# More attention chunks and the whole last x turned by DMA, with half of one FFN's second weights split again from raw

## The chip, the cores and the metric

The kernel runs on one core of one Trainium2 chip. The metric is the device time of one execution in microseconds (us), as the median of several runs.

## The reference

```python
x = A_x                                  # [1, 2048, 640], fp32
xn = layernorm(x)
qkv = (xn @ wqkv)                        # 32 heads of 20
# each position attends to itself and to 7 earlier ones, 2 apart
logits = sum(q * k[pos - 2*w]) * 20**-0.5   for w in 0..7   (masked where pos - 2*w < 0)
s = (softmax(logits) @ v) @ wo
g = silu( silu(xn @ w1) @ w2 )           # w1 640x1536, w2 1536x640
out = x + s * g
```

## The kernel before

The 2048 tokens are worked off in four groups of 512 (T = 4 tiles of 128 tokens). A group is one half of the tokens of one parity, since attention steps by two. The model width 640 is DC = 5 chunks of 128 columns, the FFN width 1536 is 12 chunks, and the heads are taken in NQ = 4 quarters of 160 columns.

Every matmul is done to fp32 accuracy: each operand is split into a high part (fp32r) and the rest (low), and three matmuls are added (high x high, low x high, high x low). So a weight unit is kept as two halves, and an activation as TH and TL (x) or OH and OL (attention output), transposed, with the contraction on the partitions.

A group passes through two phases on TensorE. The qkv phase (L960 to L962) takes quarter by quarter and chunk by chunk; one weight unit there is 4 tiles x 3 matmuls. The ffn phase has twelve up-projections (L1140 to L1142, sums in the two `rot` banks, evacuated by L1153, L1154 and L1155), twelve down-projections (L1005 and L1007, six `acc` banks, evacuated through silu into the gate by L1224), and in the middle the wo projection of the group before, whose sums L1040 multiplies with the gate; L1053 loads x again, L1054 adds it and L1056 writes the output. While a group is in its ffn phase, the x of the next is loaded (L600, and L1085 for the last use), normalized on VectorE (L607 to L619) and turned.

Attention runs beside all that on VectorE (L754 scores, L757 reduction, L770 to L783 softmax, L796 to L809 values) with help of GpSimd. Its k and v need halos, rows shifted by partitions, which SyncE (SP) copies quarter by quarter by DMA (L728), with L736 to L740 carrying rows between groups. The outputs of a group are turned in five O chunks, during the next group's qkv phase.

A chunk is turned in one of two ways. On TensorE, `split_t` transposes four tiles into a `rot` bank (L629), ScalarE writes the high part (L633, and L635 for x a whole copy), and VectorE the low part (L639). By DMA, `send` regroups the 16-bit halves of the chunk on ScalarE (L657), SP issues two DMA transposes (L662), and `join` puts the halves together on ScalarE (L670), writes the high part (L676) and the low part on VectorE (L677). The tables X_DMA and O_DMA say which chunks go by DMA for which group.

Weights come into a ring of seven slots. At its first use a unit is loaded raw in fp32 by SP (L538, into tiles XR, G or PR), split by ScalarE (L574) and VectorE (L578), and its halves are stored to DRAM (L583). Later uses load the halves through GpSimd's queue (L565).

The order of instructions on each engine comes from a list scheduler written in Python (class Weave): every operation has a cost, a due time and the tiles that it reads and writes, and the planner appends operations to the engines by these. TensorE's order is fixed by the program. `free_for(old, new)` makes the use of new names wait for that of old names where they share memory.

Of the kernel before, what the change touches and what calls it, by code (L numbers as in the profile page):

```python
# [15 lines left out]
P = 128  # L16
# [42 lines left out]
O_BACK = (), (80.0, 82.0), (80.0, 82.0), (40.0, 55.0, 60.0)  # L59
X_BY = {1: 2, 3: 0, 4: 1}  # L60
SLOW, ISSUE, SUB_LATE = 8, 2.0, 3
PACE0, PACE = -20.0, 12.0
# [3 lines left out]
STORE_Q = 1, 3  # L66
SHARED = (1, 0), (1, 2), (2, 0), (2, 2), (3, 0)
# [256 lines left out]
def local_attention_silu_ffn(ctx: ExitStack, tc: tile.TileContext, x, wqkv, wo, w1, w2, out):  # L324
# [152 lines left out]
    def store_at(u):  # L477

        return 1 + (u[0] == "wo" or u[0] == "q" and u[2] in STORE_Q)
# [29 lines left out]

    def raw_load(k):  # L510
# [12 lines left out]
        pairs = []  # L523
        if u[0] == "q":
            _, q, c = u
            whole = wqkv[c * P:(c + 1) * P, :]
            pairs.append((r.rearrange("p (k m) -> p k m", k=3), whole.rearrange("p (k m) -> p k m", k=3)[:, :, q * CQ:(q + 1) * CQ]))
        elif u[0] == "w1":
            pairs.append((r.rearrange("p (c f) -> p c f", c=DC),
                          w1.rearrange("(c p) f -> p c f", p=P)[:, :, u[1] * P:(u[1] + 1) * P]))  # L530
        else:
            m = wo if u[0] == "wo" else w2
            pairs.append((r, m[u[1] * P:(u[1] + 1) * P, :]))
        by = nc.scalar if k in BY_ACT else nc.sync

        def go():
            for to, frm in pairs:
                by.dma_start(to, frm)  # L538
        if k in BY_ACT:
            add("ACT", 0.65 * len(pairs), go, [], kr, -1, nbytes=n * P * 4)  # L540
            return
        dma(go, [], kr, n * P * 4, 1 + k if k < 2 * DC else clock[0] + 5, (0.62 if k < 2 * DC else 0.45) * len(pairs))

    def raws_due(i, k):

        while rawn[0] < len(fresh) and fresh[rawn[0]] <= i + RAW_AHEAD and raw_in.get(raw_tile(rawn[0]), -1) <= k:
            raw_load(rawn[0])
            rawn[0] += 1

    def w_load():  # L550
# [11 lines left out]
        due = clock[0]  # L562
        if what[i] == "load":
# [16 lines left out]
        if what[i] == "store":  # L580
            kept = dram.tile([P, 2, n], F32, name="half_" + "_".join(map(str, u)))
            halves[u] = kept
            dma(lambda: nc.sync.dma_start(kept, both.bitcast(F32)), [kh, kl], [("half", u)], 2 * n * P * 4, due + 25)  # L583
# [101 lines left out]

    def turn_o(c, i, by, to, at, back):
# [494 lines left out]
    def ffn_phase(g, i, ix, io):  # L1181
# [13 lines left out]
        bufs = [("buf", c, h) for c in range(DC) for h in range(2)]  # L1195
# [29 lines left out]
        if g < NG - 1:  # L1225
            turn_os(g, i, begun)

# [39 lines left out]
```

## Time and profile before

| what | value |
|---|---|
| median of the runs | 598.78 us (598.73 to 599.15) |
| profiled execution, its time | 598.41 us |
| its span | 596.3 us |
| PE, matmuls | 590.6 us busy (99%) |
| DVE | 513.3 us busy (86%) |
| ACT | 248.7 us busy (42%) |
| POOL | 168.2 us busy (28%) |
| PE L629 (chunks turned on TensorE), 20 pieces of the chain | 1.5% of the chain |
| half loads L565, w1 and w2 (640 KB each) | 72, median 7.0 us from issue to landing |

In the profile PE is TensorE, DVE is VectorE, ACT is ScalarE, POOL is GpSimd, SP is SyncE. Rows of a timeline give start, duration, engine, line, operation, output<-inputs with shapes, and in brackets how long the engine was idle before and what ended that. The span counts the profiled engines' work; the execution's own time is 2.1 us longer. TensorE ran at the full granted clock throughout.

### The profile page before, as it was taken

What the parts mean: (1) busy time and instruction counts of PE and PEld (TensorE: products, weight loads), DVE (VectorE), ACT (ScalarE), POOL (GpSimd) and SP (SyncE); (2) the same over time, 40 slices, a digit from 0 to 9 for tenths busy, and PEclk for the clock granted to TensorE, in tenths of its full rate; (3) what the DMA queues carried; (4) which work ended last, traced back from release to release, by engine and by line L of the source; (5) the groups of instructions that cost most, each with busy time, mean ns of one, the idle gap of its engine ahead of it and who ended that gap; (6) DMA issues with size and microseconds to landing.
All of it is one profiled execution on the core that took longest, in us unless ns stands there. A gap on an engine that the chain in (4) does not pass through costs nothing.

```text
span 596.3 us, 9080 instructions
## 1 busy us (share of the span) xinstructions
PE 590.6 (99%) x3443; PEld 555.9 (93%) x3443; DVE 513.3 (86%) x505; ACT 248.7 (42%) x444; POOL 168.2 (28%) x229
## 2 busy tenths in 40 slices
PE   8999999999999999999999999999999999999997
PEld 7999999999999999999999999999999999999997
DVE  6499999999799978999988996999838799998744
ACT  5437375452545223747523604443412333335230
POOL 5800102233110153442221126543121233434100
PEclk9999999999999999999999999999999999999999
DMA  9999999879999999999699999998689999797952
GB/s 295 311 295 334 296 411 402 322 252 300 271 316 326 313 257 324 239 202 239 191 319 306 303 346 304 263 208 286 211 220 283 294 320 295 227 203 215 241 185 89
DMA packets 80263, 164.21 MB, mean 275 GB/s; under 512 B 19949, under 2 KB 44237, under 8 KB 80221
## 3 DMA queue, kind: packets, MB, share of 16 engines
q1 hardware_dynamic: 60381, 83.93, 52.1%
q0 software_dynamic: 19296, 79.31, 46.5%
q8 instruction: 27, 0.44, 0.3%
q10 hardware_dynamic: 544, 0.41, 0.2%
q14 instruction: 15, 0.12, 0.1%
HBM read 107.91 MB, written 34.16 MB: 238 GB/s over the span
## 4 chain that ended last, share of the span: by engine, by line
PE 98%; DMA 0%; DVE 0%; issue 0%
PE acc L1005 23%; PE acc L1007 15%; PE acc L960 10%; PE acc L961 10%; PE acc L962 10%; PE rot L1140 9%; PE rot L1142 9%; PE rot L1141 9%; PE acc L910 2%; PE rot L629 1%; DMA xin<-in_A_x_dram 0%; PE rot L894 0%; PE rot L1123 0%; DVE st L879 0%; PE rot L853 0%; DVE gate L1091 0%
## 5 line engine op out<-in xcount | busy, mean ns | idle before, releaser
L960 PE MATMUL acc<-w,th 128*128 128x480 f32 x300 | 110.6, 369 | 0.0
L961 PE MATMUL acc<-w,tl 128*128 128x480 f32 x300 | 109.8, 366 | 0.0
L962 PE MATMUL acc<-w,th 128*128 128x480 f32 x300 | 109.8, 366 | 0.0
L1005 PE MATMUL acc<-w,sh 128*128 128x384 f32 x384 | 108.6, 328 | 0.0
L1007 PE MATMUL acc<-w,sh 128*128 128x256 f32 x384 | 104.7, 273 | 0.0
L754 DVE TENSOR_TENSOR pr<-q,kv 128x2560 f32<-128x2560 f32 x32 | 90.2, 2819 | 15.9 <-DMA kv<-carry 12.7
L796 DVE TENSOR_TENSOR pr<-q,kv 128x2560 f32<-128x2560 f32 x32 | 91.5, 2860 | 1.4 <-DVE l L757 0.5
L1140 PE MATMUL rot<-th,w 128*128 128x512 f32 x240 | 91.8, 383 | 0.0
L1141 PE MATMUL rot<-tl,w 128*128 128x512 f32 x240 | 91.0, 379 | 0.0
L1142 PE MATMUL rot<-th,w 128*128 128x512 f32 x240 | 91.0, 379 | 0.0
L757 DVE TENSOR_REDUCE l<-pr 128x128 f32<-128x2560 f32 x32 | 89.7, 2804 | 0.2
L1153 ACT ACTIVATE sh<-rot 128x512 fp32r<-128x512 f32 x48 | 28.8, 599 | 134.2 <-PE rot L1142 134.1
L565 POOL DMA_DIRECT2D w<-half_w x72 | 39.0, 542 | 156.6 <-PE acc L1007 57.6
L1007 PEld LDWEIGHTS acc<-w,sh 128*128 128x128 f32 x384 | 73.7, 192 | 0.6
L1005 PEld LDWEIGHTS acc<-w,sh 128*128 128x128 f32 x384 | 72.6, 189 | 0.6
L565 POOL DMA_DIRECT2D w<-half_q x52 | 28.0, 538 | 119.8 <-PE acc L962 74.3
L962 PEld LDWEIGHTS acc<-w,th 128*128 128x128 f32 x300 | 56.7, 189 | 4.0
L960 PEld LDWEIGHTS acc<-w,th 128*128 128x128 f32 x300 | 56.7, 189 | 3.9
L961 PEld LDWEIGHTS acc<-w,tl 128*128 128x128 f32 x300 | 56.7, 189 | 3.9
L1005 PE MATMUL acc<-w,sl 128*128 128x384 f32 x192 | 55.9, 328 | 0.0
L1155 DVE TENSOR_TENSOR sl<-sf,sh 128x512 fp32r<-128x512 f32 x48 | 39.3, 819 | 16.8 <-ACT sf L1154 16.8
L1007 PE MATMUL acc<-w,sl 128*128 128x256 f32 x192 | 52.3, 273 | 0.0
(110 smaller groups left out, 1070.0 us busy)
## 6 DMA issues: line engine op xcount, KB each, us to landing
w<-half_w POOLq DMA_DIRECT2D x72, 640.0 KB, 7.0
w<-half_q POOLq DMA_DIRECT2D x52, 480.0 KB, 5.8
half_w<-w SPq DMA_DIRECT2D x24, 640.0 KB
half_q<-w SPq DMA_DIRECT2D x20, 480.0 KB
kv<-kv SPq DMA_DIRECT2D x15, 560.0 KB
w<-half_wo POOLq DMA_DIRECT2D x10, 640.0 KB, 5.6
kv<-kv SPq DMA_DIRECT2D x15, 420.0 KB
gate<-in_B_w_dram SPq DMA_DIRECT2D x16, 320.0 KB
```

Source lines behind the costliest of these rows:

```text
L565: add("POOL", 1.0, lambda: nc.gpsimd.dma_start(both, src), [("half", u)], [kh, kl], due + 10, nbytes=2 * n * P * 4)
L754: dve(2560, lambda: nc.vector.tensor_tensor(out=PR, in0=win(qq[:, t:t + 2, :], W, 0), in1=win(kv[:, 0, t:t + 2, :], W, CQ), op=OP.mult), h ...
L757: dve(2560, lambda: nc.vector.tensor_reduce(out=l[:, t:t + 2].rearrange("p t w h -> p (t w h)"), in_=PR.rearrange("p t w (h d) -> p (t w h ...
L796: dve(2560, lambda: nc.vector.tensor_tensor(out=PR.rearrange("p t w (h d) -> p t (w h) d", d=DH), in0=e[:, t:t + 2].rearrange("p t w h -> ...
L960: nc.tensor.matmul(o, hi, vh, start=c == 0, stop=False)
L961: nc.tensor.matmul(o, lo, vh, start=False, stop=False)
L962: nc.tensor.matmul(o, hi, vl, start=False, stop=c == DC - 1)
L1005: nc.tensor.matmul(a[t][0][:, :CA].rearrange("p (m h) -> p m h", h=2), st, col_a(w), start=first, stop=last)
L1007: nc.tensor.matmul(b[t // 2][0][:, h * CB:(h + 1) * CB].rearrange("p (m h) -> p m h", h=2), st, col_b(w), start=first and h == 0, stop=las ...
L1140: nc.tensor.matmul(to, wh[:, cs], hi, start=c == 0, stop=False)
L1141: nc.tensor.matmul(to, wh[:, cs], lo, start=False, stop=False)
L1142: nc.tensor.matmul(to, wl[:, cs], hi, start=False, stop=c == DC - 1)
```

## The change

- All five chunks of the x of the last group (turned in the third group's FFN, X_DMA[2]) now go by DMA; chunks 0 and 1 went by TensorE. Their pace is moved: PACE0 for this group goes from -20 to +4.
- Four more O chunks go by DMA, sent at the end of their own group's FFN (`turn_home`, table O_HOME): chunk 2 of the second group, chunks 0, 1 and 2 of the third. (The code counts groups from 0, so these are keys 1 and 2.) They pass through pieces of XIN, the tile of x, which the next x needs afterwards: so the x loads wait for them.
- The units 6 to 11 of w2 are split again from raw at their third use (RAW_AGAIN): raw loads by SP with the two splitting instructions, where GpSimd loaded both halves.
- The tables X0_OUT to X0_BACK, `turn_first` and STORE_W2 are not used with the settings here.

```diff
-X_DMA = {1: (0, 1, 2, 3, 4), 2: (2, 3, 4)}
+X_DMA = {1: (0, 1, 2, 3, 4), 2: (0, 1, 2, 3, 4)}
 O_DMA = {1: (0, 1), 3: (0, 1, 2)}
+O_HOME = {1: {2: 5.0}, 2: {0: -9.0, 1: -6.0, 2: -3.0}}
+HOME_BACK = 20.0
-PACE0, PACE = -20.0, 12.0
+PACE0 = {1: -20.0, 2: 4.0}
+PACE = 12.0
+RAW_AGAIN = {("w2", 3): [(f,) for f in range(6, 12)]}
+AGAIN_AHEAD = 6
...
-        what.append("load" if n > at else "store" if n == at and n < again[u] else "split")
+        what.append("load" if n > at and u[1:] not in RAW_AGAIN.get((u[0], n), ()) else "store" if n == at and n < again[u] else "split")
...
+    def ahead(i):
+        return AGAIN_AHEAD if units[i][0] == "w2" and i > fresh[early] else RAW_AHEAD
...
-        while rawn[0] < len(fresh) and fresh[rawn[0]] <= i + RAW_AHEAD and raw_in.get(raw_tile(rawn[0]), -1) <= k:
+        while rawn[0] < len(fresh) and fresh[rawn[0]] <= i + ahead(fresh[rawn[0]]) and raw_in.get(raw_tile(rawn[0]), -1) <= k:
...
+    def turn_home(g, i):
+
+        todo = O_HOME.get(g, {})
+        if not todo:
+            return
+        old = [("xin", t) for t in range(T)]
+        place = [(piece(XIN, k), ("xp", k)) for k in range(DC)] + [(TURN, ("turn",))]
+        new = [k for _, p in place[:DC] for k in both(p)]
+        free_for(old, new)
+        for n, (c, at) in enumerate(todo.items()):
+            turn_o(c, i, place[2 * n], place[2 * n + 1], clock[0] + at, clock[0] + at + HOME_BACK)
+        free_for(new, old)
...
-                            if k not in O_DMA.get(g - 1, ()):
+                            if k not in O_DMA.get(g - 1, ()) and k not in O_HOME.get(g - 1, ()):
                                 o_chunk(g - 1, k, io)
...
-                    turn_x(c, ix, by, (piece(G, c), ("buf", c)), clock[0] + PACE0 + PACE * k, clock[0] + BACK[g])
+                    turn_x(c, ix, by, (piece(G, c), ("buf", c)), clock[0] + PACE0[g] + PACE * k, clock[0] + BACK[g])
...
         if g < NG - 1:
             turn_os(g, i, begun)
+            turn_home(g, i)
```

The lines move with the change: L538 becomes L545, L574 L590, L578 L594, L600 L614, L607 L621, L629 L643, L639 L653, L657 L671, L662 L676, L670 L684, L676 L690, L677 L691, L728 L762, L738 L772, L754 L788, L757 L791, L770 L804, L780 L814, L960 L994, L1040 L1074, L1056 L1090, L1085 L1119, L1140 L1174, L1153 L1187, L1224 L1261.

What it does to the order is shown at three places. The first is TensorE in the third group's qkv phase, where the second group's O chunk 2 was turned (`rot` is the transpose bank, `o` the attention output, `acc` a sum). Before:

```order
L960 MATMUL acc_114<-w_77,th_67 128x480
L961 MATMUL acc_114<-w_77,tl_73 128x480
L962 MATMUL acc_114<-w_77,th_67 128x480
L629 MATMUL rot_119<-ident,o 128x128 x4
L960 MATMUL acc_115<-w_78,th_67 128x480
L961 MATMUL acc_115<-w_78,tl_73 128x480
L962 MATMUL acc_115<-w_78,th_67 128x480
```

After:

```order
L994 MATMUL acc_114<-w_77,th_67 128x480
L995 MATMUL acc_114<-w_77,tl_73 128x480
L996 MATMUL acc_114<-w_77,th_67 128x480
L994 MATMUL acc_115<-w_78,th_67 128x480
L995 MATMUL acc_115<-w_78,tl_73 128x480
L996 MATMUL acc_115<-w_78,th_67 128x480
```

The four transposes are gone, and nothing stands in their place. All of TensorE's order differs by six such groups (twenty before, fourteen now): this one, the two of x in the third FFN, and three in the fourth group's qkv phase.

The second place is VectorE in the same phase (`q`, `kv` and `pr` belong to attention, `l`, `m` and `z` to its softmax, `st` and `mv` to the statistics of the next x in `xin`, `xr` are raw weights of wo, `tl` a chunk's low part). Before:

```order
L609 BN_AGGR mv<-st_72 128x2
L754 TENSOR_TENSOR pr<-q_97,kv_93 128x2560
L615 RECIPROCAL sd<-sd 128x4
L619 TENSOR_SCALAR xin<-xin,mv,sd 128x640 x2
L639 TENSOR_TENSOR tl_74<-rot_119,th_70 128x512
L619 TENSOR_SCALAR xin<-xin,mv,sd 128x640 x2
L578 TENSOR_TENSOR w_77<-xr_107,w_77 128x640
L578 TENSOR_TENSOR w_78<-xr_108,w_78 128x640
L578 TENSOR_TENSOR w_79<-xr_109,w_79 128x640
L757 TENSOR_REDUCE l_103<-pr 128x128
```

After:

```order
L804 TENSOR_REDUCE m_66<-l_103 128x32
L806 TENSOR_TENSOR l_103<-l_103,m_66 128x256
L788 TENSOR_TENSOR pr<-q_98,kv_94 128x2560
L691 TENSOR_TENSOR tl_74<-xin,th_70 128x512
L594 TENSOR_TENSOR w_77<-xr_107,w_77 128x640
L594 TENSOR_TENSOR w_78<-xr_108,w_78 128x640
L814 TENSOR_REDUCE z_91<-q_97 128x32
L816 RECIPROCAL z_91<-z_91 128x32
L594 TENSOR_TENSOR w_79<-xr_109,w_79 128x640
L817 TENSOR_TENSOR q_97<-q_97,z_91 128x4x64
L791 TENSOR_REDUCE l_104<-pr 128x128
L653 TENSOR_TENSOR tl_74<-rot_119,th_70 128x512
```

The statistics and the normalization of the next x have moved behind these rows, and the second quarter's scores (`q_98`, `kv_94`) have moved ahead of the O chunk (L653) that frees the first transpose bank for the up-projections.

The third place is SP's queue, first in the third group's qkv phase between the halo shifts of its first two quarters (`kv_93` and `kv_94`). Before:

```order
L728 DMA kv_93<-kv_93 14x2x480
L738 DMA kv_94<-carry_121 1x2x640
L740 DMA kv_94<-carry_121 2x2x480
L600 DMA xin<-in_A_x_dram 128x640 x4
L728 DMA kv_94<-kv_94 112x2x640
```

After:

```order
L762 DMA kv_93<-kv_93 14x2x480
L676 DMA_TRANSPOSE xin<-xin 128x4x128 x2
L772 DMA kv_94<-carry_121 1x2x640
L774 DMA kv_94<-carry_121 2x2x480
L762 DMA kv_94<-kv_94 112x2x640
```

The transposes of the home chunk now hold XIN, and the four loads of x have moved behind the last carry, ahead of the shifts of `kv_96`. Then at the end of the third group's FFN (`gate` and `turn` are the places that a chunk passes through, `xr` the raw tiles). Before:

```order
L1056 DMA out_dram<-xr_107 128x640
L662 DMA_TRANSPOSE gate<-turn 128x4x128 x2
L1053 DMA xr_108<-in_A_x_dram 128x640
L1056 DMA out_dram<-xr_108 128x640
L662 DMA_TRANSPOSE gate<-gate 128x4x128 x4
L1085 DMA xin<-in_A_x_dram 128x2x192
```

After:

```order
L676 DMA_TRANSPOSE gate<-gate 128x4x128 x2
L545 DMA xr_107<-in_B_w_dram 128x640
L1090 DMA out_dram<-xr_108 128x640
L545 DMA xr_109<-in_B_w_dram 128x640
L545 DMA xr_108<-in_B_w_dram 128x640
L676 DMA_TRANSPOSE gate<-turn 128x4x128 x2
L545 DMA xr_107<-in_B_w_dram 128x640
L545 DMA xr_108<-in_B_w_dram 128x640
L676 DMA_TRANSPOSE gate<-gate 128x4x128 x4
L772 DMA kv_93<-carry_122 1x2x640
L774 DMA kv_93<-carry_122 2x2x480
L676 DMA_TRANSPOSE xin<-xin 128x4x128 x4
```

Raw loads of w2 now stand between the transposes of x, and the home chunks' transposes follow right behind them, ahead of the first shifts of the fourth group.

More of the change, by code (lines that the diff above doesn't have):

```diff
@@ L508, in raw_tile, with raw_ap @@
         return "xr", k % 3
+    def raw_ap(u, r):
+        if u[0] == "q":
+            _, q, c = u
+            whole = wqkv[c * P:(c + 1) * P, :]
+            return r.rearrange("p (k m) -> p k m", k=3), whole.rearrange("p (k m) -> p k m", k=3)[:, :, q * CQ:(q + 1) * CQ]
+        if u[0] == "w1":
+            return r.rearrange("p (c f) -> p c f", c=DC), w1.rearrange("(c p) f -> p c f", p=P)[:, :, u[1] * P:(u[1] + 1) * P]
+        return r, (wo if u[0] == "wo" else w2)[u[1] * P:(u[1] + 1) * P, :]
     def raw_load(k):
@@ L522, in raw_load @@
         raws[i] = r, kr
[L523 to L533, printed above, removed]
+        pairs = [raw_ap(u, r)]
         by = nc.scalar if k in BY_ACT else nc.sync
@@ L562, in w_load, with keep @@
         due = clock[0]
+        def keep():
+            kept = dram.tile([P, 2, n], F32, name="half_" + "_".join(map(str, u)))
+            halves[u] = kept
+            dma(lambda: nc.sync.dma_start(kept, both.bitcast(F32)), [kh, kl], [("half", u)], 2 * n * P * 4, due + 25)
         if what[i] == "load":
@@ L580, in w_load @@
         if what[i] == "store":
-            kept = dram.tile([P, 2, n], F32, name="half_" + "_".join(map(str, u)))
-            halves[u] = kept
-            dma(lambda: nc.sync.dma_start(kept, both.bitcast(F32)), [kh, kl], [("half", u)], 2 * n * P * 4, due + 25)
+            keep()
         raws_due(i, k)
@@ L684, in turn_x, with turn_first @@
              (chunk_span("x", c, True), chunk_span("x", c)))
+    def turn_first(c, i, at, back):
+        by, to = (TL[i][:, c, :], ("lp", c)), (TH[i][:, c, :], ("hp", c))
+        free_for(t_keys(i, [c], kinds=["tl"]), both(by[1]))
+        free_for(t_keys(i, [c], kinds=["th"]), both(to[1]))
+        turn_x(c, i, by, to, at, back)
     def turn_o(c, i, by, to, at, back):
@@ L1194, in ffn_phase @@
         by_dma = X_DMA.get(g, ())
-        bufs = [("buf", c, h) for c in range(DC) for h in range(2)]
+        bufs = [("buf", c, h) for c in range(DC) for h in range(2)] if g else []
+        if not g:
+            for k, c in enumerate(by_dma):
+                turn_first(c, ix, begun + X0_OUT + X0_PACE * k, begun + X0_BACK + X0_PACE * k)
         for kind, f in plan(g):
```

4 lines of the change are left out of this document (3 added, 1 removed).

## Prediction

> **What bounds the kernel now.** I read the page's span and chain first, then TensorE's waits, because a chain that is nearly all one engine leaves only two questions: how much work that engine does, and what it ever waits for.
>
> ```profile
> span 596.3 us, 9080 instructions
> PE 98%; DMA 0%; DVE 0%; issue 0%
> ```
>
> ```profile
> PE rot L866 <- POOL ident masks.py:199: 1.4, 1, 1.4
> PE rot L894 <- DVE xin L884: 0.5, 1, 0.5
> ```
>
> 98% of the chain is TensorE (PE), and the two waits shown are both from the start. From then on PE never waits: the end moves by what is taken from PE's stream, plus any wait that the change creates. The chain also prices a chunk turned on PE. These are six of its twenty L629 pieces (start, us, what):
>
> ```profile
> 320.54 0.44 PE rot L629 x4
> ...
> 366.75 0.44 PE rot L629 x4
> ...
> 383.48 0.44 PE rot L629 x4
> ...
> 449.10 0.44 PE rot L629 x4
> 454.40 0.44 PE rot L629 x4
> 466.99 0.44 PE rot L629 x4
> ```
>
> In PE's timeline one of them looks like this:
>
> ```profile
> 320.18 0.37 PE L962 MATMUL acc<-w,th 128*128 128x480 f32 x1
> 320.38 0.60 PE L629 MATMUL rot<-ident,o 128*128 128x128 f32 x4
> 320.73 0.45 PE L960 MATMUL acc<-w,th 128*128 128x480 f32 x1
> 321.02 0.37 PE L961 MATMUL acc<-w,tl 128*128 128x480 f32 x1
> ```
>
> Durations overlap, so starts count: L962 to the next instruction takes 0.20 us, the four transposes 0.35, and the matmul behind them 0.29 instead of 0.20. 0.35 + 0.09 is the chain's 0.44.
>
> **The change, part by part.** The profiled execution took 598.41 us (span 596.3 and 2.1 around it), 0.37 below the median 598.78 of the runs; I take the sum off both alike.
>
> *Six chunks leave PE.* One O chunk at 320.54, two x chunks at 366.75 and 383.48, three O chunks at 449.10, 454.40 and 466.99. In the new order nothing else leaves PE's stream or joins it. 6 x 0.44 = 2.64 us, all on the chain, since PE had no wait that could swallow it: 598.41 - 2.64 = 595.77, and for the median 598.78 - 2.64 = 596.14.
>
> The Trainium skill (VectorE: DVE Perf Modes, The three transpose paths) gives 390 ns for a 128x128 transpose on TensorE in bf16 and 1309 ns through the DMA crossbar, and its rules for kernel authors advise TensorE wherever a PSUM destination will do, which speaks against this change. As an estimate from that page the 24 transposes would be worth 24 x 0.39 = 9.4 us; the trace has 0.44 us for four of them, so its sum is 2.64.
>
> *What takes their place.* Each chunk now costs ScalarE (ACT) a regrouping copy, two transposes on SP's queue, a joining copy, a high copy and VectorE's (DVE) subtraction. The raw half of the second weights trades six 655 KB loads on POOL's queue for six of 328 KB on SP's, plus six ACT copies and six DVE subtractions (L578). On DVE that is 6 x 0.78 = 4.7 us more (row 323.81 below); the chunks' own subtractions only change their line. Its cover is DVE's idle time, of which 12.68 us stand in one piece at 450.06. On ACT, which the page has busy for 42%, a join costs 1.36 us where a PE chunk's copies stood. Both engines are off the chain, so these cost nothing unless they come late at one of the places that follow.
>
> ```profile
> L670 ACT ACTIVATE xin<-gate 128x1024 uint16<-128x1024 uint16 x8 | 10.9, 1363 | 0.0
> ```
>
> *Place 1: attention in the third group's qkv.* DVE, in the timeline:
>
> ```profile
> 307.29 2.83 DVE L754 TENSOR_TENSOR pr<-q,kv 128x2560 f32<-128x2560 f32 x1 [1.69 <-ACT q L717]
> ...
> 317.17 0.89 DVE L607 BATCH_NORM_STATS2 st<-xin 128x6 f32<-128x320 f32 x2 [1.18 <-DMA xin<-in_A_x_dram]
> ...
> 321.11 1.14 DVE L619 TENSOR_SCALAR xin<-xin,mv,sd 128x640 f32<-128x640 f32 x2
> ...
> 323.81 1.55 DVE L578 TENSOR_TENSOR w<-xr,w 128x640 fp32r<-128x640 f32 x2
> ...
> 330.12 0.68 DVE L639 TENSOR_TENSOR tl<-rot,th 128x512 fp32r<-128x512 f32 x1
> 330.72 0.61 DVE L770 TENSOR_REDUCE m<-l 128x32 f32<-128x256 f32 x1
> ...
> 331.71 2.82 DVE L754 TENSOR_TENSOR pr<-q,kv 128x2560 f32<-128x2560 f32 x1
> ...
> 335.28 2.81 DVE L757 TENSOR_REDUCE l<-pr 128x128 f32<-128x2560 f32 x1
> 338.01 0.61 DVE L780 TENSOR_REDUCE z<-q 128x32 f32<-128x256 f32 x1
> ...
> 339.38 0.68 DVE L1155 TENSOR_TENSOR sl<-sf,sh 128x512 fp32r<-128x512 f32 x1
> ```
>
> Between 307.29 and the L639 that frees the transpose bank for the first up-projection, the new order has three L754 (2.83), three L757 (2.81), L770 and its follower (330.72 to 331.71, 0.99), one chunk subtraction (0.68), three L578 (0.78 each) and the L780 group (338.01 to 339.38, 1.37): 8.49 + 8.43 + 0.99 + 0.68 + 2.34 + 1.37 = 22.30. So L639 ends at 307.29 + 22.30 + 0.68 = 330.27. PE wants the bank here:
>
> ```profile
> 333.76 0.46 PE L1140 MATMUL rot<-th,w 128*128 128x512 f32 x1
> ...
> 360.01 0.33 PE L1005 MATMUL acc<-w,sh 128*128 128x384 f32 x1
> ```
>
> With the chunk of 320.54 gone that is 333.32, a slack of 3.05 us. The third L754 of the sum reads the second quarter's halos, which SP moves; DVE wants them at 307.29 + 2 x (2.83 + 2.81) + 0.99 = 319.56. On SP's queue:
>
> ```profile
> 296.74 4.26 SPq L728 DMA_DIRECT2D kv<-kv  x4
> ...
> 302.41 3.03 SPq L600 DMA_DIRECT2D xin<-in_A_x_dram  x4
> 308.89 3.25 SPq L728 DMA_DIRECT2D kv<-kv  x4
> ...
> 442.31 6.26 SPq L728 DMA_DIRECT2D kv<-kv  x8
> ...
> 454.90 3.70 SPq L728 DMA_DIRECT2D kv<-kv  x3
> ```
>
> ```profile
> 450.06 2.83 DVE L754 TENSOR_TENSOR pr<-q,kv 128x2560 f32<-128x2560 f32 x1 [12.68 <-DMA kv<-carry]
> ...
> 467.85 2.82 DVE L754 TENSOR_TENSOR pr<-q,kv 128x2560 f32<-128x2560 f32 x1 [1.04 <-DMA kv<-kv]
> ```
>
> From shift to reader: 450.06 - 442.31 = 7.75 and 467.85 - 454.90 = 12.95, both ended by the DMA. From 308.89 the halos are there at 316.64 to 321.84, at worst 2.28 late, inside the slack. I take no stall, because the four loads of x that stood ahead of these shifts at 302.41 are gone from there. In their place stand the two transposes of the home chunk, and what these do to other transfers is in the GB/s of the twelve microseconds from 498 on, in forty slices of 0.3 us:
>
> ```profile
> GB/s 367 384 273 222 341 375 341 393 240 281 180 120 113 60 46 19 169 271 221 0 4 9 10 364 324 495 461 358 0 0 0 68 137 17 358 358 495 341 478 341
> ```
>
> From the ninth to the thirtieth slice (6.6 us) the rate is 159 on average, beside about 360 when it runs freely: 6.6 x (1 - 159/360) = 3.7 us of transfer time per chunk. SP should issue this chunk near 302.4, and 6.6 us later is 309.0, just as the shifts begin, so I take 0 of it for the halos; the other end is all 6.6 us, and both ends go into the first rival.
>
> The Trainium skill (Advanced Engine Details and Errata, X-Bar Transpose) says that these transposes are as fast as regular DMAs, at 350 to 400 GB/s. The trace disagrees, with 159; by the page the first rival would not exist.
>
> *Place 2: the next x.* Its loads now follow the last carry of the third qkv, at about 329.7 in place of 302.41. Latency there was 317.17 - 302.41 = 14.76 to the last tile's reader; the nearest other one is the 7.75 above. So x is complete between 337.5 and 344.5. By the new order DVE wants the last tile at 330.27 plus three statistics (1.1 each with their aggregate), an L796 (2.8) and an L639 (0.68): 337.1. The stall is 0.4 to 7.4. What waits behind it is L1040, which frees PE's six sums ahead of the L1005 at 360.01:
>
> ```profile
> 354.36 3.14 DVE L1040 TENSOR_TENSOR gate<-acc,gate 128x384 f32<-128x384 f32 x6
> ```
>
> L639 to L1040 took 354.36 - 330.12 = 24.24. It loses one L754 and L757 (5.64), L770 and the L780 group (2.36), and gains four statistics (4.4) and L619 for four tiles (2.3): 22.94, so L1040 starts at 330.27 - 0.68 + 22.94 = 352.5. PE uses the third sum 0.16 after the first, so three of the six pieces (1.57) must end by 360.17 - 0.88 (two chunks less): start by 357.7, slack 5.2. The wait on PE is therefore 0 to 2.2 us. I take 0, since the reader at 317.17 sat behind four loads and four shifts at once, and the new loads do not.
>
> *Place 3: the end of the third FFN.* Three more joins (two of them in the last 10 us) stand on ACT ahead of L1224, which empties the sums that the next qkv's first matmul fills:
>
> ```profile
> 427.12 0.49 ACT L1224 ACTIVATE gate<-acc 128x384 f32<-128x384 f32 x1 [1.48 <-PE acc L1005]
> ```
>
> ```profile
> 429.50 0.37 PE L960 MATMUL acc<-w,th 128*128 128x480 f32 x1
> ```
>
> 429.50 - 427.12 - 0.49 = 1.89 of slack, and 1.48 of waiting ahead; the two joins, about 2 us each, would have to be over 1.89 late, so their last transposes would have to land after 425. SP can issue these once the last raw weight has found a free XR buffer. I take nothing for it.
>
> *The home chunks of the third group* go through SP ahead of the shifts at 442.31. Weights keep a lead of six units of twelve matmuls, 6 x 12 x 0.20 = 14.4 us. While five chunks were turned (241 to 275 us) a load took 11.2 us in place of the page's 7.0:
>
> ```profile
> w<-half_w POOLq DMA_DIRECT2D x7, 640.0 KB, 11.2
> ```
>
> ```profile
> w<-half_w POOLq DMA_DIRECT2D x72, 640.0 KB, 7.0
> ```
>
> That still fits. If it pushed the halos back by 6.6 us, the 12.68 us of DVE idle time ahead of 450.06 would come to 19 instead, and the attention behind would have to catch up in its own waits.
>
> **The rivals.** First, *the halos come late behind a turned chunk* (slower). It decides where the shift-to-reader time in the third qkv passes 10.67 + 3.05 + 2.64 = 16.4 us. With 12.95 plus 3.7 it is 16.65: 598.9, no change. With 12.95 plus 6.6 it is 19.55: PE stalls 5.8, net +3.2, 602.0; the middle is 600.4. For it: 12.95 was measured without any transposes, and one queue carries both. Against it: the chunk should be through when the shifts start. Second, *x comes late at place 2*, or the joins at place 3: 596.14 + 0 to 2.2 (place 2), up to 598.3, and a similar amount at place 3; the middle is 597.6. For it: 14.76 was measured. Against it: 5.2 us of slack. That the six groups stay on PE is excluded by the order, which has fourteen left of twenty.
>
> **How the numbers follow.** 0.55 for 596.1 with no new wait (its own range 595.6 to 596.6), 0.22 for late x or late joins (596.6 to 599), 0.23 for late halos (598.9 to 602). This kernel's runs lie within 0.1%, and 0.2%, 1.2 us, is about what can be told from no change: faster is below 597.6, slower above 600.0. Of the second case 0.08 is faster and 0.14 is the same; of the third 0.05 is the same and 0.18 slower. Faster 0.55 + 0.08 = 0.63, same 0.19, slower 0.18. The range runs from 595.6 to 599.6, which leaves out most of the third case.
>
> **What the profile after would show.** Right: fourteen L629 pieces of 0.44 in the chain, a PE share of 98%, TensorE's waits still the two of the start, a span near 593.7. The first rival: a wait of TensorE at the first up-projection of the third group (L1140's new line) on DVE, with DVE itself waiting for kv by DMA near 319. The second: a wait of the first down-projection (L1005) on L1040, or of the fourth qkv's first matmul on L1224. What would make me wrong besides: weights late in their ring while chunks are turned, which would show as TensorE waiting for w.

## The result and the profile after

| | before | changed |
|---|---|---|
| median of the runs | 598.75 us (598.63 to 599.15) | 607.95 us (602.27 to 616.82) |
| ratio | | 1.0116, 95% interval 1.0082 to 1.0150 |
| profiled execution (span) | 598.41 (596.3) | 616.82 (615.0) |

In this measurement the changed kernel is 1.2% slower, and its time has become uncertain: four executions spread over 14.6 us where the kernel before spreads over 0.5. Medians and ranges here hold all executions, but a ratio leaves out those that took over 1.5% longer than the fastest of their kernel, and so the profiled one, the longest of the four. Two repeats with a profile each stand with the experiments; over all sixteen executions of the changed kernel the median is 602.96, and thirteen are above 600.

The span and the chain from the page of the changed kernel, and TensorE's waits:

```profile
span 615.0 us, 9076 instructions
PE 83%; DMA 7%; DVE 4%; SPq 2%; issue 1%; ACT 1%; DVEq 0%; ACTq 0%
```

```profile
PE acc L994 <- ACT gate L1261: 9.1, 1, 9.1
PE rot L1174 <- DVE tl L653: 6.7, 1, 6.7
PE rot L900 <- POOL ident masks.py:199: 1.4, 1, 1.4
PE rot L928 <- DVE xin L918: 0.7, 1, 0.7
```

TensorE is no longer 98% of the chain. Two long waits are new. Its own work did shrink as forecast; in the groups by line (count, busy us, mean ns) there are 36 + 20 transposes, fourteen chunks of four, where there were twenty:

```profile
L643 PE MATMUL rot<-ident,o 128*128 128x128 f32 x36 | 5.4, 273 | 0.0
L643 PE MATMUL rot<-ident,xin 128*128 128x128 f32 x20 | 3.0, 273 | 0.0
```

What the waits cost beyond themselves stands in the view by windows (start:end, length, busy time of PE, PEld, DVE, ACT and POOL with counts, granted clock, DMA share, GB/s):

```profile
284.00:293.20 9.20, 0.19 (x2) 0.00 (x0) 2.31 (x2) 2.34 (x4) 2.16 (x3) 0.73 1.39 132
293.20:298.00 4.80, 4.74 (x12) 4.00 (x13) 4.73 (x4) 2.14 (x7) 0.00 (x0) 0.50 1.11 176
298.00:303.00 5.00, 5.00 (x26) 4.62 (x25) 3.71 (x8) 3.68 (x4) 1.06 (x2) 0.96 0.44 133
345.00:352.20 7.20, 0.52 (x5) 0.28 (x3) 7.17 (x10) 1.58 (x5) 0.53 (x1) 0.82 0.86 284
352.20:357.00 4.80, 4.76 (x13) 3.87 (x14) 4.76 (x7) 2.52 (x3) 0.00 (x0) 0.56 1.01 357
357.00:362.00 5.00, 5.00 (x36) 4.92 (x35) 4.86 (x13) 2.67 (x4) 1.06 (x2) 1.00 1.04 365
```

Behind each long wait TensorE works 4.8 us at 0.50 and 0.56 of its clock, which is 2.4 and 2.1 us lost. The Trainium skill (TensorE: Matmul & The Clock Gate, Part 1) says that the clock falls to half after an idle window of about 3.4 us; the trace agrees with the half, but not with the length, since a wait of 2.5 us was enough in one of the runs below. The sum for this execution: 596.3 - 2.64 = 593.7, plus 9.1 and 6.7, plus 4.5 is 614.0, of 615.0.

The second wait (6.7) is the prediction's first rival. SP, then ACT, then DVE, in the timeline of the changed kernel:

```profile
313.06 3.49 SPq L676 DMA_TRANSPOSE xin<-xin  x2
...
320.84 4.42 SPq L762 DMA_DIRECT2D kv<-kv  x4
```

```profile
327.62 1.36 ACT L684 ACTIVATE xin<-xin 128x1024 uint16<-128x1024 uint16 x1 [6.62 <-DMA xin<-xin]
```

```profile
342.04 2.83 DVE L788 TENSOR_TENSOR pr<-q,kv 128x2560 f32<-128x2560 f32 x1 [9.53 <-DMA kv<-carry]
```

The home chunk's transposes were issued at 313.06 and its join could start only at 327.62, 14.6 us later. The second quarter's shifts, issued at 320.84 while they were still under way, reached their reader at 342.04, after 21.2 us. VectorE stands still for 9.53 us and L653, nine rows behind, frees the bank too late. (The bracket names a carry, a row that is copied between groups; by the semaphores in the trace the wait ended with the last of the four shifts, which landed at 341.82.)

The first wait (9.1) lies at the end of the second group's FFN, in a stretch that the change does not touch: up to about 300 us every engine has the instructions of the kernel before, in the same order. ACT waits there for the last turned chunk of x, and L1261 stands behind its join:

```profile
290.82 1.34 ACT L684 ACTIVATE xin<-gate 128x1024 uint16<-128x1024 uint16 x1 [10.30 <-DMA gate<-gate]
292.20 0.63 ACT L690 ACTIVATE th<-xin 128x512 fp32r<-128x512 f32 x1
292.73 2.59 ACT L1261 ACTIVATE gate<-acc 128x384 f32<-128x384 f32 x6
```

In the kernel before, ACT's timeline has the same last join over at 279.7, and ACT has time to spare ahead of L1224, the line that is L1261 now:

```profile
279.07 0.64 ACT L676 ACTIVATE th<-xin 128x512 fp32r<-128x512 f32 x1
281.55 0.49 ACT L1224 ACTIVATE gate<-acc 128x384 f32<-128x384 f32 x1 [1.84 <-PE acc L1005]
```

Whether this wait belongs to the change was the first question for the experiments.

### The profile page after: what moved, and what is told of

The parts are those of the page before. It is cut to its first block, busy times and chain, and to the rows that moved or that the text cites. A ratio compares the mean times of both kernels' runs of the same rounds, so it can differ in the third digit from the quotient of the medians.

```text
span 615.0 us, 9076 instructions
## 1 busy us (share of the span) xinstructions
PE 593.1 (96%) x3419; PEld 557.0 (91%) x3419; DVE 515.3 (84%) x511; ACT 262.7 (43%) x458; POOL 163.0 (26%) x223
## 4 chain that ended last, share of the span: by engine, by line
PE 83%; DMA 7%; DVE 4%; SPq 2%; issue 1%; ACT 1%; DVEq 0%; ACTq 0%
PE acc L1039 19%; PE acc L1041 12%; PE acc L994 9%; PE acc L996 9%; PE acc L995 9%; PE rot L1174 8%; PE rot L1175 7%; PE rot L1176 7%; DMA gate<-gate 4%; DMA kv<-kv 3%; PE acc L944 2%; SPq L676 2%; DVE l L791 1%; PE rot L643 1%; DMA xin<-in_A_x_dram 1%
## 5 line engine op out<-in xcount | busy, mean ns | idle before, releaser
L994 PE MATMUL acc<-w,th 128*128 128x480 f32 x300 | 111.5, 372 | 9.1 <-ACT gate L1261 9.1
L1039 PE MATMUL acc<-w,sh 128*128 128x384 f32 x384 | 108.4, 328 | 0.0
L788 DVE TENSOR_TENSOR pr<-q,kv 128x2560 f32<-128x2560 f32 x32 | 90.3, 2821 | 21.3 <-DMA kv<-carry 14.0
L1174 PE MATMUL rot<-th,w 128*128 128x512 f32 x240 | 92.8, 387 | 6.7 <-DVE tl L653 6.7
L791 DVE TENSOR_REDUCE l<-pr 128x128 f32<-128x2560 f32 x32 | 89.7, 2803 | 0.2
L1187 ACT ACTIVATE sh<-rot 128x512 fp32r<-128x512 f32 x48 | 28.7, 598 | 131.2 <-PE rot L1176 131.2
L581 POOL DMA_DIRECT2D w<-half_w x66 | 35.8, 542 | 162.0 <-PE rot L1176 58.1
L1039 PEld LDWEIGHTS acc<-w,sh 128*128 128x128 f32 x384 | 72.6, 189 | 0.6
L994 PEld LDWEIGHTS acc<-w,th 128*128 128x128 f32 x300 | 57.4, 191 | 13.5 <-ACT gate L1261 9.3
L996 PEld LDWEIGHTS acc<-w,th 128*128 128x128 f32 x300 | 57.3, 191 | 4.3
L1174 PEld LDWEIGHTS rot<-th,w 128*128 128x128 f32 x240 | 45.9, 191 | 12.9 <-DVE tl L653 7.0
L1039 PE MATMUL acc<-w,sl 128*128 128x384 f32 x192 | 55.9, 328 | 0.0
L1189 DVE TENSOR_TENSOR sl<-sf,sh 128x512 fp32r<-128x512 f32 x48 | 36.8, 767 | 22.3 <-ACT sf L1188 22.2
```

The lines of the kernel that those rows point to most:

```text
L581: add("POOL", 1.0, lambda: nc.gpsimd.dma_start(both, src), [("half", u)], [kh, kl], due + 10, nbytes=2 * n * P * 4)
L788: dve(2560, lambda: nc.vector.tensor_tensor(out=PR, in0=win(qq[:, t:t + 2, :], W, 0), in1=win(kv[:, 0, t:t + 2, :], W, CQ), op=OP.mult), h ...
L791: dve(2560, lambda: nc.vector.tensor_reduce(out=l[:, t:t + 2].rearrange("p t w h -> p (t w h)"), in_=PR.rearrange("p t w (h d) -> p (t w h ...
L994: nc.tensor.matmul(o, hi, vh, start=c == 0, stop=False)
L996: nc.tensor.matmul(o, hi, vl, start=False, stop=c == DC - 1)
L1039: nc.tensor.matmul(a[t][0][:, :CA].rearrange("p (m h) -> p m h", h=2), st, col_a(w), start=first, stop=last)
```

## The experiments

Theory A: the second group's home chunk delays the halos, and that is the loss. Theory B: the loss is the end of the second FFN. Theory C: every added chunk stalls TensorE where it meets weight loads or halos. Theory D, formed after the first eight runs, joins them: waits for late DMA at several places that come and go, each long one with the low clock behind it. Edits are given against the changed kernel; medians are in us, with the range of the executions.

**The changed kernel again, twice (after_again, after_third).** No edit.

> The changed kernel once more, to see which of its waits come back. Theory A: what costs is the second group's home chunk, whose two transposes stand on SP's queue ahead of the second quarter's halos; then TensorE's wait on L653 near 340 us (6.7 us in the first profile) is there again, and times lie at 602 or above. Theory B: what costs is the end of the second group's FFN, where the order is that of the kernel before and the first profile has a wait of 9.1 us on L1261; then that wait comes and goes between executions, and the times spread from 602 to 617 as before. Both may hold: then the lowest times have the first wait alone.

> The changed kernel a third time, for one more profile. Theory D: the loss is a sum of TensorE waits for late DMA at up to four places (end of the second FFN, start of the third, its weights near 394 us, start of the fourth), each of which comes and goes between executions; a wait of over 3.5 us costs about 2.5 us more by a clock of 0.5 behind it. Then span = 593.7 + the waits shown beyond the start + 2.5 for each long one, within 1 us. A single cause (theory A) would show the same wait as one of the first two profiles.

Measured: 603.71 (597.67 to 608.80) beside 598.68, and 602.76 (597.34 to 606.20) beside 599.30, ratio 1.0032 (0.9982 to 1.0082). The waits in the two profiles:

```profile
PE acc L1039 <- DMA w<-half_w: 2.2, 1, 2.2
...
PE rot L1174 <- DVE tl L653: 0.5, 1, 0.5
```

```profile
PE rot L1174 <- DVE tl L653: 3.8, 1, 3.8
...
PE acc L1039 <- DMA w<-half_w: 0.9, 1, 0.9
```

Spans 597.4 and 602.3. The wait at the second FFN's end is in neither, that on L653 in all three. Theory D's sums: 593.7 + 2.7 = 596.4 (1.0 short), and 593.7 + 4.7 + 2.5 = 600.9 (1.4 short, not within the 1 us I gave). The best executions, 597.34 and 597.67, are 1.1 to 1.4 us below the 598.75 of the kernel before: part of the gain comes out when little goes wrong. After the short wait of 2.2 us the clock stayed up:

```profile
523.40:528.00 4.60, 4.60 (x30) 4.47 (x31) 4.46 (x6) 3.04 (x3) 3.67 (x5) 1.00 1.11 419
```

The halos of the second quarter in the three profiles, from the shifts' issue to their reader: 309.00 to 323.93 (14.93), 309.29 to 327.53 (18.24), 320.84 to 342.04 (21.20); waits on L653: 0.5, 3.8, 6.7. The prediction's own formula, delay - 10.67 - 3.05, gives 1.2, 4.5 and 7.5: the slope is right, 0.7 to 0.8 too high each. So the halos' time of arrival sets this wait; whether the chunk sets the time of arrival is another question, which two of the runs below bear on.

**Without the second group's home chunk (no_home1).**

```diff
-O_HOME = {1: {2: 5.0}, 2: {0: -9.0, 1: -6.0, 2: -3.0}}
+O_HOME = {2: {0: -9.0, 1: -6.0, 2: -3.0}}
```

> The changed kernel without the second group's home chunk (chunk 2 is turned on TensorE again; the x loads of the last group stand early again). Theory A: the wait on L653 is gone, 598.75 - 5 x 0.44 = 596.6. Theory B: the wait at the end of the second FFN is as frequent as in the changed kernel, so times spread from 596.6 to about 610.

614.86 (610.68 to 630.51), ratio 1.0244 (1.0207 to 1.0282): slower still, so theory A alone falls. The waits: L1174 on a weight 4.3, L1174 on L653 3.8 (at 491, now in the fourth group), L1174 on L1188 1.4.

**The home chunk alone (home1_only), and the same 23 us later (home1_28).** X_DMA, PACE0 and RAW_AGAIN as before the change.

```diff
+O_HOME = {1: {2: 5.0}}      # first run
+O_HOME = {1: {2: 28.0}}     # second run
```

> Only the second group's home chunk is added to the kernel before. Theory A: the wait on L653 is there by itself: 598.75 - 0.44 + 4 to 7 = 602 to 605. Theory B: 598.3 where the second FFN does not stall, with a spread of several us above.

> As the run with only the second group's home chunk, but sent 23 us later, so that its transposes stand on SP's queue behind the second quarter's halos (ahead of the third's). Theory A: the wait of L1174 on L653 at the start of the third FFN is gone or moves behind the third quarter: 598.3 to 600. Theory B: it is the second FFN's end that costs, which is not touched: a spread of 598 to 616 as in that run.

The first: 606.56 (598.14 to 616.84), ratio 1.0041 (0.9999 to 1.0083) over five of its ten executions; its profile holds the 9.0 us wait at the second FFN's end and 0.2 on L653, with the halos at their reader after 14.66 us. The second: 610.46 (605.59 to 612.68), ratio 1.0160 (1.0077 to 1.0242). With the chunk behind them the halos take 12.98 us (309.36 to 322.34), and there is no wait on L653. TensorE waits later instead:

```profile
PE acc L1039 <- DVE gate L1074: 6.0, 1, 6.0
PE acc L994 <- DMA w<-half_q: 2.2, 1, 2.2
```

The first of these is the prediction's place 2. The chunk goes through XIN, the tile of x, and now holds it longer: its join starts at 333.04, the loads of the next x go out at 346.01 (327.39 in after_again), VectorE stands still for them, and L1074 behind them is late.

```profile
362.30 0.89 DVE L621 BATCH_NORM_STATS2 st<-xin 128x6 f32<-128x320 f32 x2 [9.25 <-DMA xin<-in_A_x_dram]
```

So moving the chunk moved the wait to another input.

**The x loads moved, no chunk (xlate1).** All chunks and raw loads as before the change; the last group's x loads wait for the fourth quarter.

```diff
-behind = [("kv", XQ, 0)] if g else []
+behind = [("kv", 3 if g == 2 else XQ, 0)] if g else []
```

> The kernel before with only the loads of the last group's x moved behind the third qkv's last carry, where the changed kernel has them; no chunk moves. If late x costs by itself (place 2 of the prediction: 0 to 2.2 us), a wait of L1039 on L1074 near 360 us and 599 to 603; if not, 598.8.

598.81 (598.48 to 611.59), ratio 1.0001 (0.9961 to 1.0040). So late, x costs nothing that can be told. And two of the ten executions are at 606.6 and 611.6; the profile is of the longer one and shows why:

```profile
PE acc L994 <- ACT gate L1261: 8.8, 1, 8.8
```

That is the wait at the second FFN's end, in a kernel that turns the same chunks as the one before. Beside it the kernel before itself had three executions of nineteen at 605.6 to 609.6, of which there is no profile. So this wait needs none of the change: the code that both kernels share there can stall. That the first profile of the changed kernel caught it may have been bad luck. Whether the change makes it more frequent is not shown. In home1_only, with the same order up to there, seven of ten executions are above 604, against five of 83 of the kernel before in all measurements, but only one of the seven has a profile.

The same trace bears on the halos. Only the first quarter's shifts and the carries stand ahead of the second quarter's shifts here, no chunk and no load of x, and they still reach their reader after 14.86 us, as late as in after_again:

```profile
320.11 4.51 SPq L762 DMA_DIRECT2D kv<-kv  x4
```

```profile
334.97 2.82 DVE L788 TENSOR_TENSOR pr<-q,kv 128x2560 f32<-128x2560 f32 x1 [3.83 <-DMA kv<-kv]
```

In the kernel before, with four loads of x ahead, they were later still. Issued at 308.89, they landed at 328.79 by the trace's semaphores, 19.9 us later. SP's waits between 308 and 335 us show it, since the load at 328.86 had to wait for a shift:

```profile
SPq L538 <- DMA kv<-kv: 0.9, 1, 0.9
```

Nobody else noticed, because VectorE's order had the second quarter's L754 only at 331.71. The changed order wants them at about 320. That the chunk delays the halos is therefore not shown for the short delays (14.66 and 14.93, beside 14.86 without it); for 18.24 and 21.20 it may.

**The three home chunks of the third group alone (home2_only).** X_DMA, PACE0 and RAW_AGAIN as before the change. TensorE's order is that of before up to 449 us, VectorE's up to 381.

```diff
+O_HOME = {2: {0: -9.0, 1: -6.0, 2: -3.0}}
```

> Only the third group's three home chunks are added to the kernel before; up to about 425 us the order is that of before. Theory C (each added chunk stalls TensorE where it meets weight loads or halos): waits only in the fourth group, after 430 us; without one 598.7 - 1.3 = 597.4, with one of 3 to 9 us and the low clock behind it 603 to 609. Theory B (the end of the second FFN stalls in any program but the one before): a wait of about 9 us near 285 us in the profile or in most executions, 605 to 612.

601.90 (599.51 to 604.71), ratio 1.0056 (1.0037 to 1.0075). Its profile has one new wait, 3.9 us of L1174 on L653 at 483, after VectorE waited for halos (the bracket names x, but by the trace's semaphores the shifts of 454.76 ended the wait, landing at 468.38):

```profile
468.50 2.83 DVE L788 TENSOR_TENSOR pr<-q,kv 128x2560 f32<-128x2560 f32 x1 [3.10 <-DMA xin<-in_A_x_dram]
...
482.61 0.68 DVE L653 TENSOR_TENSOR tl<-rot,th 128x512 fp32r<-128x512 f32 x1
```

Place 1 of the prediction repeats itself a group later. The halos took 13.74 us to their reader, only 0.79 more than in the kernel before. By these rows the larger part is VectorE's new order: the L639 that frees this bank stood at 476.78 before, ahead of the next scores at 478.90; now L653 stands behind the scores of 479.86. Whether the transposes or the final x loads that they push into this phase delay the halos was not tried apart.

**The two x chunks alone (x_only), with the raw loads (x_raw_only), and the raw loads alone (raw_only).**

```diff
+O_HOME = {}                          # all three
+RAW_AGAIN = {}                       # x_only
+X_DMA, PACE0 as before the change    # raw_only
```

> Only the two x chunks by DMA with the later pace, all of w2 loaded as halves. Theory C: more weight bytes beside five transposed chunks than in the run with the raw loads (606.9 median, a wait of 3.7 us of the up-projection on a weight at 393 us), so waits there are as long or longer: 605 to 612. If the raw loads were the cause of that wait, it is gone here: 597.9.

> Only the two x chunks by DMA and the raw loads of half of w2; no home chunks. Theory A: no wait, 598.75 - 2 x 0.44 = 597.9. Theory B: a spread of some us above that. If the raw loads or the late joins at the end of the third FFN cost, a wait of the fourth qkv's first matmul on L1261 of up to 2 us: 598 to 600.

> Only the raw loads of half of w2 at their third use are added to the kernel before; no chunk moves, TensorE's order is that of before. Theory C: no chunk is added and two megabytes of weights are saved, so 598.7 with no wait. If the raw loads' wait for XR buffers on SP's queue is what costs, a wait of L1039 on w or of L994 on L1261 between 400 and 430 us: 600 to 606. Theory B: a wait near 285 us, 605 to 612.

x_only: 603.26 (599.35 to 606.62), ratio 1.0063 (1.0029 to 1.0097). x_raw_only: 606.94 (602.70 to 610.83), 1.0134 (1.0083 to 1.0185). raw_only: 599.81 (599.56 to 602.42), 1.0018 (1.0005 to 1.0031), with 0.7 us on L653 at 481. The x chunks stall TensorE on a weight at 394 us, here in x_only, and by 3.7 us in x_raw_only:

```profile
394.88 0.80 PE L1174 MATMUL rot<-th,w 128*128 128x512 f32 x1 [5.13 <-DMA w<-half_w]
```

The weights issued around that time took, median from issue to landing, first in x_only (issued from 373 to 377) and then in the kernel before (372 to 395):

```profile
w<-half_w POOLq DMA_DIRECT2D x3, 640.0 KB, 21.6
```

```profile
w<-half_w POOLq DMA_DIRECT2D x8, 640.0 KB, 9.0
```

Like for like, from 373 to 377, the kernel before has 9.6, x_raw_only 20.4 and no_home1 21.0. That is over the lead of 14.4. The likely reason is on SP's queue of x_only: two chunks are sent back to back (four transposes between 364 and 374), where the kernel before has one there and the next at 386.

```profile
364.33 2.86 SPq L676 DMA_TRANSPOSE gate<-turn  x2
...
369.65 4.73 SPq L676 DMA_TRANSPOSE gate<-gate  x2
```

It can't be the whole reason. In after_again the same two chunks are sent at 364.24 and 371.74, and the load of this window took 10.8 us; in the kernel before two chunks go back to back at 386 without a wait.

**The x chunks spaced (x5_16_12), and the banks freed earlier on top (x5_oata).**

```diff
-PACE0 = {1: -20.0, 2: 4.0}
+PACE0 = {1: -20.0, 2: 16.0}          # both, on x_only
+ O_AT in the fourth group: chunks 2, 3, 4 after (2, 2), (2, 4), (3, 1)   # x5_oata
```

> As the run with only the two x chunks by DMA, but the five chunks are sent 12 us later each (16 instead of 4 us from the wo projection, same pace), so that the first two are no longer turned back to back. If two chunks together hold back the weights (21.6 us from issue to landing instead of 9.5, lead 14.6), the wait on a weight near 394 us is gone and the time is 597.9; the last joins come later, so a wait of L994 on L1261 near 428 us is the risk, 600 to 604. If the sum of bytes and transposes is the cause, the wait stays: 600 to 606.

> The run with the x chunks spaced (x5_16_12), with the fourth group's last three O chunks moved earlier in TensorE's stream (after units (2,2), (2,4), (3,1)), so that VectorE frees both banks ahead of the second half of the second quarter's scores. In x5_16_12 the only long wait was that of L1174 on L653 at 486 us (4.6). Theory D with that wait as the term: it is gone, and the usual execution is at 598.8 - 0.88 = 597.9 or a little above; then this version is the one that beats both. If the lateness reaches TensorE by another way: 600 to 606 with a wait elsewhere.

606.59 (605.01 to 608.42), ratio 1.0106 (1.0022 to 1.0191), and 605.60 (604.22 to 606.49), 1.0094 (1.0064 to 1.0124). The wait on the weight at 394 is gone, as expected of two chunks apart (the loads of 373 to 377 took 5.3 us). In its place came 4.6 us on L653 at 486, and when that was taken away, 3.1 us of L994 on L751 at 472:

```profile
PE rot L1174 <- DVE tl L653: 4.6, 1, 4.6
```

```profile
PE acc L994 <- ACT q L751: 3.1, 1, 3.1
```

With the last chunks' joins later, the final x loads go out at 429.81 instead of 408.20, just ahead of the fourth group's halos; whether that caused the new waits was not tried.

**Two chunks fewer in the second FFN (after_x3).**

```diff
-X_DMA = {1: (0, 1, 2, 3, 4), ...
+X_DMA = {1: (2, 3, 4), ...
```

> The changed kernel with two chunks fewer turned by DMA in the second group's FFN (chunks 0 and 1 go back to TensorE there, +0.88 us). Theory B: the wait at the end of that FFN cannot come, and the spread shrinks to what the later places give; the lowest executions are at 597.0 to 598.6 and the median falls below 601. Theory C: the later places stall as before, median 602 to 608.

606.74 (605.04 to 608.84), ratio 1.0139 (1.0110 to 1.0169). No wait at the second FFN's end in its profile, but 2.5 us of L994 on L751 at 325 and 1.7 of L1174 on L1188 at 403: the later places stall, as theory C had it. TensorE's timeline and the windows show that 2.5 us were enough for the low clock, for some 4 us:

```profile
325.37 0.47 PE L994 MATMUL acc<-w,th 128*128 128x480 f32 x1 [2.53 <-ACT q L751]
```

```profile
325.50:329.50 4.00, 4.00 (x12) 3.45 (x13) 3.90 (x7) 2.74 (x8) 0.00 (x0) 0.57 1.03 374
330.00:333.00 3.00, 3.00 (x16) 2.81 (x15) 2.93 (x8) 0.74 (x1) 0.00 (x0) 1.00 1.05 211
```

**L653 taken from behind the late halos.** First by the planner's weight for a transpose, which moved the whole plan, then by TensorE's own order alone.

```diff
-SLOW, ISSUE, SUB_LATE = 8, 2.0, 3
+SLOW, ISSUE, SUB_LATE = 16, 2.0, 3    # after_s16; 24 in after_s24
```

```diff
-for k in O_AT.get((q, c), ()):
+for k in ({(2, 2): (3,), (2, 4): (4,)} if g > 1 else O_AT).get((q, c), ()):   # after_oat2; (2, 4) and (3, 2) in after_oat
```

> The changed kernel with one number of the planner doubled: a DMA transpose counts for twice the time (SLOW 16 for 8), so that it expects the halos behind turned chunks later. The same chunks go by DMA; on VectorE the O chunk whose L653 frees the first bank now stands ahead of the second quarter's scores (L788) in the third and in the fourth group. Theory D, with the waits on L653 as the main term: these waits are gone, and most executions lie at 596 to 599; the end of the second FFN still stalls in some. If the halos' lateness itself is what TensorE feels in the end, the wait moves to L1074 in the middle of the FFN and the time stays at 601 to 605.

> As the run before it, with the transposes counted three times (SLOW 24): both remaining O chunks of the third group's qkv stand 18 rows ahead of the second quarter's scores. Theory D: no wait on L653, 596 to 599. Against it: the attention is put off, and L1074 or the next x comes late: a wait of L1039 on L1074 near 365 us and 599 to 604.

> The changed kernel, with the two O chunks that TensorE still turns in the third and fourth group moved earlier in its own stream (after units (2,2) and (2,4) of the qkv phase in place of (3,2) and (3,4)), so that VectorE frees both banks ahead of the second quarter's late scores in the third group, and the first bank ahead of them in the fourth. No chunk, byte or queue changes. The replanned runs could not show this, since their whole plan moved. Theory D with the waits on L653 as the main term: none of them is left, the usual execution lies at 596.1 to 598.5, a few at 605 to 612 by the end of the second FFN. If the lateness reaches TensorE by another way: 601 to 605 with a wait on L1074 or on a weight.

> The same with the two chunks at (2,4) and (3,2): both of the third group's L653 stay behind the second quarter's first scores, but 7 and 4 rows earlier than in the changed kernel. Theory D: about 5 us more slack than the changed kernel at the first bank, so waits of the size of the first profile (6.7) shrink to 0 to 2 and stay free of the low clock: 596 to 600.

after_s16 632.37 (ratio 1.0540, 1.0461 to 1.0619) and after_s24 654.44 (1.0874, 1.0796 to 1.0952): the waits on L653 shrank to 0.7 and to nothing, but L1039 waits 6.5 us on L594 in the one, and in the other 12.6 on L590, with 17.0 of L994 on L1261; too much moved to conclude from them. after_oat2: 612.08 (603.90 to 619.71), 1.0177 (1.0095 to 1.0258); after_oat: 605.77 (600.57 to 608.12), 1.0130 (1.0091 to 1.0169). Neither has a wait on L653 left. They wait elsewhere, after_oat2 first, then after_oat:

```profile
PE acc L1041 <- ACT q L751: 3.9, 1, 3.9
...
PE acc L1039 <- DMA w<-half_w: 1.3, 1, 1.3
```

```profile
PE rot L1174 <- ACT sf L1188: 1.9, 1, 1.9
PE acc L1039 <- DMA w<-half_w: 1.8, 1, 1.8
```

In after_oat2 ACT stood 11.42 us in front of a raw weight of wo that came late, with the evacuations of the sums queued behind it:

```profile
338.52 0.74 ACT L590 ACTIVATE w<-xr 128x640 fp32r<-128x640 f32 x1 [11.42 <-DMA xr<-in_A_wo_dram]
```

My expectation that 596 to 599 would come back was wrong: with L653 out of the way, TensorE waits elsewhere. No version that I ran beats the kernel before, though single executions of the changed kernel do.

## Why the prediction was wrong

- *Six chunks leave TensorE, 2.64 us.* Right: fourteen groups are left, and the two fastest executions come out 1.1 to 1.4 us below 598.75; the full 2.64 was never seen.
- *The first rival's place and price.* Right in place, sign and slope (0.5, 3.8 and 6.7 us at L653 for delays of 14.93, 18.24 and 21.20). What failed is the step that kept it out of the sum: "From 308.89 the halos are there at 316.64 to 321.84, at worst 2.28 late, inside the slack. I take no stall", and behind it "I take 0 of it for the halos". Shift to reader was put at 7.75 to 12.95 us, from another group. It took 14.47 to 22.13 in the six profiles with the chunk ahead in which the reader waited, and 12.98 and 14.86 in the two without. The prediction's own slack ends at 13.72 (10.67 + 3.05), so 14.86 makes a stall without any chunk. The kernel before had these shifts land after 19.9 us; this did not show, because no reader waited.
- *The chunk's own time, 6.6 us.* Too small. The issue time was right where nothing had stalled before (301.28 and 301.52 for 302.4), but issue to join took 11.0, 10.7 and 14.6 us in the three profiles of the changed kernel, so the chunk was still under way when the shifts began. The 6.6 was the length of a dip in one GB/s row, while SP's queue held nothing but that chunk. The row does not show that much: in seven of the slices next to nothing moved (0 to 10 GB/s), which does not tell slowed transfers from none under way. The mean of 159 belongs to the tenth to the thirty-first slice, not to the ninth to the thirtieth, which have 170. And 16.65 in the rival's sum gives 599.1, not 598.9.
- *"That still fits", for the weights' lead of 14.4 us.* Wrong for the x chunks in three profiles (20.4 to 21.6 us in x_only, x_raw_only and no_home1, with waits of 3.7 to 5.1), but not in those of the changed kernel, which have no wait there. I had the load beside five chunks at 11.2 us as a median, and the lead has to hold for the slowest one.
- *The home chunks of the third group.* They had no term. By themselves they cost a wait of 3.9 us and the low clock behind it (home2_only), by the rows there most of it from VectorE's new order.
- *The price of a wait.* Too small. I added waits one for one; behind a wait of 6.7 and one of 9.1 us another 2.1 and 2.4 us went to the half clock, behind one of 2.5 still 1.7 (4.0 x (1 - 0.57)), so what I had as "no change" (a stall that eats the gain) ends slower.
- *Place 2, late x.* Right: nothing, in xlate1 and in the three profiles of the changed kernel. It does come, with 6.0 us, when x goes out later still (home1_28).
- *Place 3, late joins at the third FFN's end.* Right in the profiles of the changed kernel: no wait of L994 on L1261 there.
- *One trace as the measure of slack.* The wait at the second FFN's end, in unchanged code, was in nobody's sum. With 1.84 us of idle time ahead of L1224 in the trace of before it looked safe, yet xlate1, with the same order up to there, stalls for 8.8 us. That the first profile met it is not what the prediction got wrong. A forecast of DMA arrivals from one execution can be off by several us here.

What stays open: why the second FFN stalls, and whether more often with the change; how much of the halos' delay is the chunk's, and whether by its hold on the DMA engines or its place ahead on SP's queue; why weights took 20 to 22 us beside the two x chunks in three profiles, and 8 to 11 in others with the same chunks. Three of the changed kernel's sixteen executions have a profile, and their waits and low clocks account for their spans to within 1.4 us; what the others waited for is not known.

## What to carry to other kernels

When one engine is 98% of the chain, taking work from it pays only if what replaces it, and the new order of the other engines, still bring this engine's inputs in time; price the replacement at the slowest arrival seen, not the median, and add the clock's price to any wait of about 2.5 us or more. Before a row that reads a transfer is moved forward in an engine's order, find out when its data land: a reader that never waits hides a late arrival. Count what is in flight beside a new transfer and what is next on its queue. If a first profile shows a stall in code that the change left alone, profile again before explaining it.

## What the runs showed of the hardware

- After a wait of 2.2 us TensorE's granted clock stayed at 1.00; after one of 2.5 it was 0.57 for 4 us, and after waits of 6.7 and 9.1 it was 0.56 and 0.50 for 4.8 us. In all profiles but after_s16 and after_s24, where waits stand close together, the seven waits of 1.3 to 2.2 us left it at 1.00, and each of the fifteen of 2.5 us and more was followed by 0.50.
- One chunk's two DMA transposes took 10.0 to 14.6 us from issue to the join (home1_only and the three profiles of the changed kernel), and 19.2 in home1_28.
- The shifts of one quarter took 13.0 us (home1_28) to 22.1 us (after_oat2) from issue to a waiting reader; with four loads of x ahead on the queue they landed after 19.9 us (the kernel before).
- Executions of one and the same program differ by up to 20 us (610.68 and 630.51 in no_home1). Of the 83 executions of the kernel before, 74 lie between 598.2 and 600.5; one took 892.09.
